# Decoded weights kept in a DRAM scratch for the paired tokens, and another order of the seven products

## The chip, the cores and the metric

The kernel runs on one NeuronCore of a Trainium2 chip. The metric is the time of one execution on the device in microseconds (us).

## What is computed

Three blocks follow one another. The inputs of the first are float32; the weights of the other two are float64 and are carried to the chip as pairs of 32-bit words, so each 128x512 block of them is 512 KB.

```python
# 16 heads (2 x 8), 768 rows, head dim 64
mask   = q_bucket[:, :, :, None] == k_bucket[:, :, None, :]   # buckets: signs of 6 projections
scores = np.where(mask, 0.125 * q @ k^T, -1e9)
x = softmax(scores) @ v                  # -> x: 1536 tokens x 512
a = x @ w1; b = x @ w2                   # 512 -> 1024 each
x = ((a * b) @ w3) @ w_out               # -> 512
g = x @ w_gate; val = x @ w_val          # 512 -> 1536 each
out = (silu(g) * val) @ w_out2           # -> 512
```

Every product is made nearly float32-exact from three matmuls: both factors are split into a high and a low half (fp32r), and `split_mm` (L248) adds high x high, high x low and low x high. A tile of 128 x 1024 columns holds the high half (columns 0 to 511) and the low half (512 to 1023).

## The kernel before

The order of the work on every engine is made by a planner (`Plan`, L57). Each piece of work is an op with a cost for each engine that may do it, a priority, the ops it waits for (`deps`), the ops that must have been started first (`after`), and counted resources that it takes and gives back (`acq`, `rel`: `W` for slots of 128 x 1024, `F` for single PSUM banks, `two` for pairs of banks, `st` for small temporaries, `D`). The planner walks through modelled time, and the program is then written out in that order, engine by engine; the semaphores come from the tiles that the instructions read and write. DMAs are issued on SP, in order, except for the casts of keys and queries on POOL; the planner lets a load start only while its modelled DMA queue is no more than 4 us deep. Matmuls outside the attention ("fill") are chained in one fixed order by `fill_op` (L821).

Weights: `decode` (L329) loads a raw block and turns the float64 bits into float32 in three steps on ACT or POOL (`e`, `l`, `s`: L341, L347, L353, recorded in the helper at L255 or L257) and a join on DVE (L360). `piece` (L381) then writes the high half (ACT first) and the low half (POOL first, L262) into a slot.

Tokens come in three blocks of 512. Block 0 goes its own way; blocks 1 and 2 are paired and handled by seven instead of eight products of half-size blocks (Strassen-Winograd). The stages in order of time:

- Attention, until about 308 us; w3 x w_out is folded into one matrix `WP` beside it (tiles `wps`).
- First mixture for block 0 (tiles `f`, `fs`; L942), with `w12f` pieces, partly beside the attention.
- Second mixture for block 0, the items stage (tiles `m` and `acc`; L923 to L938 and `stage2`): 12 items of two pieces of gate and value weights and one of output weights (`w2x`), 24 + 12 matmuls each.
- The paired tokens: `pair(1, ...)`, some 465 to 608 us, then `pair(2, ...)`, to the end.

In `pair` (L1221) four (first mixture) or six (second) steps `jp` each take two sets `z` of weights (for the two factors) from `wset` (L1125). A set loads and decodes two raw blocks again, forms the four sums s1 to s4 in place of words that are no longer needed (L1140 to L1145), and splits A, C, B (512 columns) and D (256). `xset` makes the fourteen token operands once for each stage. `PROD` (L1214) names the weight, its column and the token operand of each product; each has two halves `q` of three matmuls. Products 1 and 2 share bank `a`, 6 has `b`; 5 and then 3 use half 0 of the two-bank tile `cd`, 7 and then 4 its half 1. `after` (L1293) adds the evictions: `u` is a copy of `a` on ACT after product 1; the sums after 6, 5, 7, 3 and 4 are DVE operations at L1308 (`v` is that of product 5), each read from PSUM and added to what went before. `some()` puts one unit of the second layer (three matmuls, `pacc_...` or `acc`) between products. The order of products in all steps but the first is the list at L1507.

For the second mixture 24 more pieces (`wo2p_j`, `wo2q_j`, L1232 to L1238) load and decode the output weights, twice.

Slots go round through a first-in first-out list (`slot`, `drop`, L222 to L230).

Of the kernel before, what the change touches and what calls it, by code (L numbers as in the profile page):

```python
# [31 lines left out]
N_DEC_MOE, N_SA_MOE, N_OT = 1, 0, 2  # L32
N_D, N_ST = 3, 4
P_OUT, P_SPLIT, P_T, P_X2, N_GATE = -3, -2, -1, -2.5, 6
# [137 lines left out]
def moe_after_bucket_attention(ctx: ExitStack, tc: tile.TileContext, qk, vv, pp, cst, w12, w3t, w_out, wgv, wo2, out):  # L172
# [24 lines left out]
    def c_pool_mul(cols):  # L197
# [6 lines left out]
            "W": NSLOT - 2 - 2 * X_W - WP_W, "C": 0, "ot": 0, "R": N_R, "sums": N_SUM,  # L204
            "XT": 0, "D": 0, "st": 0, "G": 0,
        }
# [613 lines left out]

    def fill_op(name, cost, fn, deps, prio, acq=(), rel=()):  # L821
        fill_prev[0] = op(name, [("PE", cost, fn)], [*deps, fill_prev[0]], prio, acq=acq, rel=rel)
        return fill_prev[0]
# [40 lines left out]

    def stage1(key, kind, tb, wk, wdep, keep, dropx=False, late=False):

# [4 lines left out]
        for z, kc in zk:  # L871
# [57 lines left out]
    def first_stage(n):  # L929
        kind, tb, j = items[n]  # L930
        if (kind, j) not in cache:
            srcs = [(w12 if kind == 1 else wgv)[j, z] for z in range(2)] + ([wo2[j]] if kind == 2 else [])
            names = [f"w{kind}x{n}_{z}" for z in range(len(srcs))]
            cache[(kind, j)] = names, [piece(a, b, P_DEC) for a, b in zip(names, srcs)]
        used[n] = cache[(kind, j)]
        if not keep[n]:
            del cache[(kind, j)]
        return stage1(f"m{n}", kind, tb, *used[n], keep[n], n == N - 1, n == 0)  # L938


    half_done = {}
    for half in range(2):  # L942
        cdone = []
        for j in range(4 * half, 4 * half + 4):
            wk = [f"w12f_{j}_{z}" for z in range(2)]
            wd = [piece(wk[z], w12[j, z], P_DF) for z in range(2)]
            for z in range(2):
                loads[z - 2].after.append(sc[min(NTL - 1, int(F_GATE[0] + (2 * j + z) * F_GATE[1]))])
            cdone.append(stage1(f"f{j}", 1, 0, wk, wd, False))
        oj = [(o_, jj) for o_ in range(4) for jj in range(4)]  # L950
# [56 lines left out]
    tail = [o for os_ in xdone.values() for o in os_]  # L1007
    sw = op("switch", [("NONE", 0.0, switch)], tail, -50, rel=[("W", NSLOT_MOE), ("ot", N_OT), ("dec", N_DEC_MOE), ("D", N_D), ("st", N_ST)])

    def stage2(n, cdep):  # L1010
# [11 lines left out]
        for o_ in range(4):  # L1022
# [24 lines left out]
            deps = [cdep, wp_done[j] if kind == 1 else used[n][1][2], sw]  # L1047
            o = fill_op(f"s2_{n}_{o_}", C3, go, deps, nextp(), acq=[("two", 1)] if first and at[o_][1] == 0 else [], rel=rel)
            if not last:
# [47 lines left out]

    def raw2(key):
        return f(env["raw" + key]).rearrange("p (a b) -> p a b", b=2)

    def hilo(name, src, dst, deps, prio, acq=(), rel=(), make=None, done=None, n=512, engines=("ACT", "POOL", "DVE")):
# [22 lines left out]

    def wset(key, srcs):  # L1125


        oa = decode(key + "a", srcs[0], P_DEC, acq=(("W", 3),))
        ob = decode(key + "b", srcs[1], P_DEC, acq=(("W", 2), ("D", 1)))

        def add(out_, a, b, alu):
            def make(eng):
                return lambda: eng.tensor_tensor(out=out_(), in0=a(), in1=b(), op=alu)

            return [("DVE", d_dve(256), make(DVE)), ("POOL", d_pool(256), make(POOL))]

        def v(side, word, half):
            return lambda: raw2(key + side)[:, 256 * half : 256 * half + 256, word]

        a11, a12, a21, a22 = v("a", 1, 0), v("a", 1, 1), v("b", 1, 0), v("b", 1, 1)  # L1140
        s1, s3, s2, s4 = v("b", 0, 1), v("b", 0, 0), v("a", 0, 0), v("a", 0, 1)
        o1 = op("s1" + key, add(s1, a21, a22, ALU.add), [ob], P_DEC, port=BOTH)
        o2 = op("s2" + key, add(s2, s1, a11, ALU.subtract), [o1, oa], P_DEC, port=BOTH)
        o4 = op("s4" + key, add(s4, a12, s2, ALU.subtract), [o2], P_DEC, port=BOTH)
        o3 = op("s3" + key, add(s3, a11, a21, ALU.subtract), [oa, ob], P_DEC, port=BOTH)  # L1145

        def whole(x):
            return lambda: (env[x + key][:, 0:512], env[x + key][:, 512:1024])

        def blocks():  # L1150
            t = env["wB" + key]
            return tuple(t[:, c : c + 512].rearrange("p (b a) -> p b a", b=2) for c in (0, 512))

        def d_tile():
            env["wD" + key] = pools["m"].tile([128, 512], F32R, tag="D", name="D" + key, bufs=N_D)

        got = {}
        got["A"] = hilo("A" + key, lambda: raw2(key + "a")[:, :, 1], whole("wA"), [oa], P_DEC, make=lambda: slot("wA" + key))
        got["C"] = hilo(
            "C" + key, lambda: raw2(key + "a")[:, :, 0], whole("wC"), [o4, got["A"]], P_DEC, make=lambda: slot("wC" + key),  # L1160
            done=lambda: drop("raw" + key + "a"), rel=[("W", 1)],
        )
        got["B"] = hilo(
            "B" + key, lambda: raw2(key + "b")[:, 256:512, :].rearrange("p a b -> p b a"), blocks, [o1, ob], P_DEC,
            make=lambda: slot("wB" + key),
        )
        got["D"] = hilo(
            "D" + key, lambda: raw2(key + "b")[:, 0:256, 0], lambda: (env["wD" + key][:, 0:256], env["wD" + key][:, 256:512]),
            [o3, got["B"]], P_DEC, make=d_tile, done=lambda: drop("raw" + key + "b"), rel=[("W", 1)], n=256,
        )  # L1170
        return got

    def xset(kind, deps, gate, prio):
# [40 lines left out]
    PROD = {  # L1214
        1: ("A", 0, "B11"), 2: ("A", 256, "B21"), 3: ("C", 256, "B22"), 4: ("B", 256, "T4"),
        5: ("B", 0, "T1"), 6: ("C", 0, "T2"), 7: ("D", 0, "T3"),
    }
    FREES = {2: "A", 3: "C", 4: "B", 7: "D"}
    cd = [None, None, None]

    def pair(kind, nj, xdep, lead, gate, prio):  # L1221
# [8 lines left out]
        for jp in range(njp):  # L1230
            for z in range(2):
                w_of[jp, z] = wset(f"{kind}_{jp}_{z}", [(w12 if kind == 1 else wgv)[2 * jp + m, z] for m in range(2)])  # L1232
            if kind == 2:
                for j in (2 * jp, 2 * jp + 1):
                    wo_of[j] = piece(f"wo2p_{j}", wo2[j], P_DEC)
        if kind == 2:
            for j in range(nj):
                wo_of[j, 2] = piece(f"wo2q_{j}", wo2[j], P_DEC)  # L1238

        def prod(jp, z, p):  # L1240
# [5 lines left out]
            for q in range(2):  # L1246

                def go(q=q):
# [8 lines left out]
                    w, x = env[f"w{wn}{key}"], env[f"X{kind}{xn}{q}"]  # L1257
                    n = 256 if wn == "D" else 512
                    c = c0 + 128 * q
                    split_mm(ps, w[:, c : c + 128], w[:, n + c : n + c + 128], x[:, 0:512], x[:, 512:1024], begins and q == 0, q == 1, not begins)  # L1260
                    if q == 1 and p in FREES:
                        (env.pop if p == 7 else drop)(f"w{FREES[p]}{key}")
                    if jp == njp - 1 and z == 1:
# [16 lines left out]
                if q == 1 and p in FREES:  # L1280
                    rel = [("D", 1)] if p == 7 else [("W", 1)]
                if jp == njp - 1 and z == 1:
# [322 lines left out]
```

## Time and profile before

| what | value |
| --- | --- |
| median of 3 runs | 826.59 us (825.54 to 827.94) |
| the profiled execution: its time | 828.18 us |
| its span, first to last instruction | 826.4 us |
| mean granted TensorE clock | 0.993 |
| busy, share of the span: PE, weight loads, DVE, ACT, POOL | 93%, 76%, 72%, 75%, 44% |
| DMA | 107.87 MB, 131 GB/s over the span; written to HBM 3.19 MB |

Busy time of TensorE runs to the modelled end of each matmul, and successive matmuls overlap: a 128x512 matmul has a duration of 0.39 us, while its successor in a full stream starts 0.23 us after it. Time lost on TensorE is therefore read from start to start, or from the idle time of its weight loads (PEld), which run ahead of the matmuls. DMA share is the mean busy share of the 16 DMA engines.

### The profile page before, as it was taken

How to read it: one execution, taken by the hardware profiler on the slowest of the kernel's cores; microseconds unless marked ns; L12 is line 12 of the kernel's file. 1: busy time of each engine (PE TensorE's matmuls, PEld its weight loads, DVE VectorE, ACT ScalarE, POOL GpSimd, SP SyncE). 2: the span in 40 equal slices, each digit the busy share in tenths (PEclk: the TensorE clock that was granted, in tenths of full speed). 3: DMA queues.
4: the chain of work that ended last, by engine and by line, in shares of the span. 5: the costliest groups of instructions: out<-in, count | busy, mean ns of one | idle time of the engine just before them, and what ended most of it. 6: DMA issues, size and time to landing. Idle time of an engine off the chain costs nothing.

```text
span 826.4 us, 11593 instructions
## 1 busy us (share of the span) xinstructions
PE 770.3 (93%) x3888; PEld 625.7 (76%) x3888; DVE 598.3 (72%) x1014; ACT 618.4 (75%) x1105; POOL 361.3 (44%) x355
## 2 busy tenths in 40 slices
PE   7998999999999999999999979999997998998897
PEld 5886888888878897877888757677775676666686
DVE  6888878897789884676944657676866677776682
ACT  6988999987889897999778855455855666585681
POOL 3577667674755635652223112224014543333340
PEclk9999999999999999999999999999999999999999
DMA  6785956764566418642254152213142223223311
GB/s 204 171 220 136 225 159 147 159 179 123 142 175 160 126 50 320 204 151 74 75 180 154 52 182 73 76 52 103 51 153 78 101 102 102 102 102 128 128 51 52
DMA packets 35844, 107.87 MB, mean 131 GB/s; under 512 B 7060, under 2 KB 9236, under 8 KB 35784
## 3 DMA queue, kind: packets, MB, share of 16 engines
q1 hardware_dynamic: 33544, 96.11, 37.8%
q0 software_dynamic: 2240, 11.01, 6.6%
q8 instruction: 31, 0.51, 0.3%
q14 instruction: 29, 0.24, 0.1%
HBM read 97.85 MB, written 3.19 MB: 122 GB/s over the span
## 4 chain that ended last, share of the span: by engine, by line
PE 60%; ACT 14%; DVE 14%; issue 5%; POOL 3%; DMA 2%; SPq 1%; POOLq 0%; DVEq 0%; ACTq 0%
PE cd L249 6%; PE cd L251 4%; PE cd L250 4%; PE T L611 4%; DVE v L1308 3%; ACT dec_w2x L255 2%; PE pacc_two L249 2%; PE pacc_two L251 2%; PE pacc_two L250 2%; PE av L680 2%; PE av L681 2%; PE S L582 2%; PE a L249 2%; DVE sl_G L1308 2%; PE a L250 2%
## 5 line engine op out<-in xcount | busy, mean ns | idle before, releaser
L262 DVE TENSOR_TENSOR P<-T,P 128x768 fp32r<-128x768 f32 x96 | 90.9, 954 | 18.0 <-ACT P L615 16.9
L589 DVE TENSOR_SCALAR_CACHE_REDUCE ms<-S 128x768 f32<-128x768 f32 x96 | 91.4, 952 | 15.6 <-PE S L583 6.5
L602 ACT ACTIVATE ms<-ms,mx 128x768 f32<-128x768 f32 x96 | 89.8, 936 | 10.4 <-DVE mx L596 9.8
L615 ACT CAST P<-T 128x768 fp32r<-128x768 f32 x96 | 76.1, 796 | 7.2 <-PE T L611 4.9
L611 PE MATMUL T<-cs,ms 128*128 128x128 f32 x576 | 79.1, 276 | 2.4 <-DVE ms L589 1.3
L582 PE MATMUL S<-KQ 128*128 128x512 f32 x192 | 68.8, 362 | 7.2 <-DVE ms L589 3.2
L680 PE MATMUL av<-P,VP 128*128 128x256 f32 x288 | 74.4, 292 | 0.7 <-ACT P L615 0.4
L611 PEld LDWEIGHTS T<-cs,ms 128*128 128x128 f32 x576 | 65.5, 141 | 9.8 <-ACT P L615 2.4
L681 PE MATMUL av<-P,VP 128*128 128x256 f32 x288 | 71.6, 283 | 0.8 <-DVE P L262 0.8
L583 PE MATMUL S<-KH,QL 128*128 128x512 f32 x192 | 60.9, 340 | 0.7 <-DVE QL L507 0.7
L680 PEld LDWEIGHTS av<-P,VP 128*128 128x128 f32 x288 | 54.6, 190 | 2.5 <-ACT tt L691 1.4
L681 PEld LDWEIGHTS av<-P,VP 128*128 128x128 f32 x288 | 54.8, 190 | 1.7 <-DVE P L262 1.2
L582 PEld LDWEIGHTS S<-KQ 128*128 128x128 f32 x192 | 36.3, 189 | 17.8 <-DVE ms L589 5.6
L262 POOL TENSOR_TENSOR sl_w2x<-sl_raww2x,sl_w2x 128x512 fp32r<-128x512 f32 x19 | 25.2, 1330 | 43.4 <-ACT sl_w2x L255 43.4
L360 DVE SCALAR_TENSOR_TENSOR sl_raww2x<-dec_w2x,dec_w2x 128x512 uint32<-128x512 uint32 x36 | 26.8, 756 | 22.8 <-ACT dec_w2x L255 19.4
L255 ACT ACTIVATE dec_w2x<-sl_raww2x 128x512 f16<-128x512 f32 (+1 forms) x57 | 40.8, 732 | 2.2 <-DVE sl_raww2x L360 1.6
L583 PEld LDWEIGHTS S<-KH,QL 128*128 128x128 f32 x192 | 36.5, 190 | 6.1 <-DVE QL L507 1.1
L249 PE MATMUL m<-sl_X,sl_w2x 128*128 128x512 f32 x96 | 38.0, 396 | 2.5 <-ACT sa_m L893 2.5
L1336 ACT COPY u<-a 128x512 f32<-128x512 f32 x20 | 11.7, 586 | 35.5 <-PE a L251 35.4
L250 PE MATMUL m<-sl_X,sl_w2x 128*128 128x512 f32 x96 | 38.1, 397 | 0.0
L251 PE MATMUL m<-sl_X,sl_w2x 128*128 128x512 f32 x96 | 38.0, 396 | 0.0
L714 POOL TENSOR_TENSOR tt<-tt 128x256 f32<-128x256 f32 x24 | 18.1, 755 | 24.3 <-ACT tt L691 18.2
(334 smaller groups left out, 2488.5 us busy)
## 6 DMA issues: line engine op xcount, KB each, us to landing
sl_raww2x<-in_wgv_dram SPq DMA_DIRECT2D x24, 512.0 KB, 3.5
KQ<-in_qk_dram POOLq DMA_DIRECT2D x28, 384.0 KB, 6.1
sl_raww<-in_w3t_dram SPq DMA_DIRECT2D x16, 512.0 KB, 5.2
sl_raww12f<-in_w_dram SPq DMA_DIRECT2D x16, 512.0 KB, 5.7
sl_raww2x<-in_wo_dram SPq DMA_DIRECT2D x12, 512.0 KB, 4.7
sl_rawwo2p<-in_wo_dram SPq DMA_DIRECT2D x12, 512.0 KB, 3.4
sl_rawwo2q<-in_wo_dram SPq DMA_DIRECT2D x12, 512.0 KB, 4.0
kqraw<-in_qk_dram SPq DMA_DIRECT2D x28, 192.0 KB, 3.4
```

Source lines behind the costliest of these rows:

```text
L249: PE.matmul(ps, a_hi, b_hi, start=first, stop=False, skip_group_check=more)
L250: PE.matmul(ps, a_hi, b_lo, start=False, stop=False, skip_group_check=more)
L251: PE.matmul(ps, a_lo, b_hi, start=False, stop=last, skip_group_check=more)
L262: eng.tensor_tensor(out=out_, in0=a, in1=b, op=ALU.subtract)
L582: PE.matmul(ps[:, c0:c1], a[:, 0, qs], a[:, 1, c0:c1], start=True, stop=False)
L583: PE.matmul(ps[:, c0:c1], q[:, qs], k[:, c0:c1], start=False, stop=True)
L589: DVE.tensor_scalar(out=env[f"ms{s}"], in0=ps[:, 0:S], scalar1=-BIG, scalar2=None, op0=ALU.max, op1=ALU.max, accum_out=env[f"mx{s}"][:, 0:1],)
L602: ACT.activation(p, p, AF.Exp, bias=m[:, 1:2], scale=0.125, accum_out=env[f"sums{hh}"][:, qt : qt + 1])
L611: PE.transpose(ps[:, c * 128 : c * 128 + 128], p[:, c * 128 : c * 128 + 128], ident)
L615: ACT.copy(env[f"P{n}"][:, kk, 0:6], env[f"T{s}"][:, 0:S].rearrange("p (c q) -> p c q", c=6))
L680: PE.matmul(ps[:, 0:256], vab, p[:, :, c], start=c == 0, stop=False)
L681: PE.matmul(ps[:, 0:256], vab, p[:, :, 6 + c], start=False, stop=c == 5)
```

## The change

`piece` gets a `save` name: once the low half is written, SP stores the whole decoded slot (512 KB) into a DRAM scratch tile. The pieces of the first mixture for block 0 (16) and of the items stage (36) are saved; the last matmul that reads such a slot is planned after its store has been issued. `wset` no longer decodes: `fetch` loads the two saved tiles as A and B, two full sums high + low are formed in one slot F, the four sums of the set are made in place on its quarters, and F's halves are split as P (s2, s4) and Q (s3, s1). `C` and `D` go; a set now has four slots A, B, P, Q. The 24 output-weight pieces of the second mixture become 24 fetches. There are seven `st` temporaries in place of four and the three `D` tiles. In the steps after the first, product 2 moves behind product 5, and units come after 6, 2, 7 and 3 (before: 6, 5, 7 and 3).

```diff
-N_D, N_ST = 3, 4
+N_ST = 7
...
+    saved = {}
+
-    def piece(key, src, prio, late=()):
+    def piece(key, src, prio, late=(), save=None):
...
+        if save is not None:
+
+            def put():
+                env["dram" + save] = dpool.tile([128, 1024], F32, name="dram" + save)
+                SP.dma_start(out=env["dram" + save], in_=f(env[key]))
+
+            saved[save] = op("sv" + key, [("SP", 0.48, put)], [o6], -4, xfer=1.4)
         return o6
...
-            o = fill_op(f"{key}_{z}{kc}", C3, go, [wdep[z], *xdeps(kc, tb)], nextp(), acq=[("F", 1)] if kc == 0 else [], rel=rel)
+            o = fill_op(f"{key}_{z}{kc}", C3, go, [wdep[z], *xdeps(kc, tb)], nextp(), acq=[("F", 1)] if kc == 0 else [], rel=rel, after=[saved[sv[z]]] if kc == 3 else [])
...
-            cache[(kind, j)] = names, [piece(a, b, P_DEC) for a, b in zip(names, srcs)]
+            cache[(kind, j)] = names, [piece(a, b, P_DEC, save=f"{kind}_{j}_{z}") for z, (a, b) in enumerate(zip(names, srcs))]
...
-            wd = [piece(wk[z], w12[j, z], P_DF) for z in range(2)]
+            sv = [f"1_{j}_{z}" for z in range(2)]
+            wd = [piece(wk[z], w12[j, z], P_DF, save=sv[z]) for z in range(2)]
...
-    def wset(key, srcs):
-        oa = decode(key + "a", srcs[0], P_DEC, acq=(("W", 3),))
-        ob = decode(key + "b", srcs[1], P_DEC, acq=(("W", 2), ("D", 1)))
...
+    def fetch(key, save, acq, prio=P_DEC):
+        def load():
+            SP.dma_start(out=f(slot(key)), in_=env["dram" + save])
+
+        o = op(
+            "ld" + key, [("SP", 0.48, load)], [saved[save]], prio, acq=[("W", acq)], xfer=1.9, after=[last_load[0], *load_after],
+            queue=Q_LOAD,
+        )
...
+    def wset(key, a, b):
+        got = {"A": fetch("wA" + key, a, 3), "B": fetch("wB" + key, b, 2)}
+        def full(x, h):
+            def make(eng):
+                def go():
+                    if "F" + key not in env:
+                        slot("F" + key)
+                    w = f(env[f"w{x}{key}"])
+                    eng.tensor_tensor(out=f(env["F" + key])[:, HALF[h]], in0=w[:, 0:512], in1=w[:, 512:1024], op=ALU.add)
...
+            return op(f"f{x}{key}", [("POOL", d_pool(512), make(POOL)), ("DVE", d_dve(512), make(DVE))], [got[x]], P_DEC, port=BOTH)
...
+        fa, fb = full("A", 0), full("B", 1)
+        o1 = add("s1", 3, 2, 3, ALU.add, [fb])
+        o3 = add("s3", 2, 0, 2, ALU.subtract, [fa, o1])
+        o2 = add("s2", 0, 3, 0, ALU.subtract, [o1, o3])
+        o4 = add("s4", 1, 1, 0, ALU.subtract, [o2])
...
+        got["P"] = hilo("P" + key, lambda: f(env["F" + key])[:, HALF[0]], whole("wP"), [o4], P_DEC, make=lambda: slot("wP" + key))
+        got["Q"] = hilo(
+            "Q" + key, lambda: f(env["F" + key])[:, HALF[1]], whole("wQ"), [o1, o3, got["P"]], P_DEC, make=lambda: slot("wQ" + key),
+            done=lambda: drop("F" + key), rel=[("W", 1)],
+        )
...
     PROD = {
-        1: ("A", 0, "B11"), 2: ("A", 256, "B21"), 3: ("C", 256, "B22"), 4: ("B", 256, "T4"),
-        5: ("B", 0, "T1"), 6: ("C", 0, "T2"), 7: ("D", 0, "T3"),
+        1: ("A", 0, "B11"), 2: ("A", 256, "B21"), 3: ("P", 256, "B22"), 4: ("B", 256, "T4"),
+        5: ("Q", 256, "T1"), 6: ("P", 0, "T2"), 7: ("Q", 0, "T3"),
     }
-    FREES = {2: "A", 3: "C", 4: "B", 7: "D"}
+    FREES = {2: "A", 3: "P", 4: "B", 7: "Q"}
...
-                    wo_of[j] = piece(f"wo2p_{j}", wo2[j], P_DEC)
+                    wo_of[j] = fetch(f"wo2p_{j}", f"2_{j}_2", 1)
...
-                order = [(z, p) for z in range(2) for p in (1, 6, 2, 5, 7, 3, 4)]
+                order = [(z, p) for z in range(2) for p in (1, 6, 5, 2, 7, 3, 4)]
             for z, p in order:
                 prod(jp, z, p)
-                if p in (6, 5, 7, 3):
+                if p in (6, 2, 7, 3):
                     some()
```

## Rows read from the trace of the kernel before

**Rows 1.** Timeline, items stage: start us, us, engine, line, operation, tiles, [idle <-releaser].

```profile
449.01 0.39 PE L249 MATMUL m<-sl_X,sl_w2x 128*128 128x512 f32 x1
...
452.94 0.77 DVE L262 TENSOR_TENSOR sl_w2x<-sl_raww2x,sl_w2x 128x512 fp32r<-128x512 f32 x1 [0.93 <-ACT sl_w2x L255]
...
457.17 0.39 PE L249 MATMUL m<-sl_X,sl_w2x 128*128 128x512 f32 x1
```

**Rows 2.** Busy time by stretch: us, then busy (count) each, PEclk, DMA share, GB/s.

```profile
310.00:441.00 131.00, 127.34 (x558) 104.11 (x557) 80.93 (x111) 109.32 (x187) 55.06 (x48) 0.99 0.49 166
498.00:580.00 82.00, 77.31 (x318) 58.04 (x317) 56.45 (x91) 43.62 (x75) 23.86 (x23) 1.00 0.22 71
636.00:785.00 149.00, 135.31 (x547) 101.01 (x546) 106.86 (x164) 99.06 (x168) 56.29 (x55) 0.99 0.32 110
```

**Rows 3.** Waits of weight loads, 498:580, then 636:785: total us, times, longest.

```profile
PEld cd L249 <- DVE v L1308: 5.7, 7, 1.2
PEld cd L249 <- DVE sl_G L1308: 3.8, 6, 1.2
PEld cd L249 <- DVE t L1308: 1.6, 3, 0.5
PEld cd L249 <- issue: 1.2, 2, 0.6
...
PEld cd L249 <- DVE v L1308: 12.7, 15, 1.2
PEld cd L249 <- DVE sl_G L1308: 6.6, 10, 1.2
PEld cd L249 <- DVE t L1308: 4.7, 5, 1.2
```

**Rows 4.** Timeline of TensorE and DVE, one short wait and one long.

```profile
559.90 0.39 PE L251 MATMUL pacc_two<-sl_C1p,sl_WP 128*128 128x512 f32 x1
560.48 0.47 PE L249 MATMUL cd<-sl_X1T,D 128*128 128x512 f32 x1 [0.20 <-DVE v L1308]
...
642.51 0.39 PE L251 MATMUL cd<-sl_X2T,D 128*128 128x512 f32 x1
642.93 0.69 DVE L1308 TENSOR_TENSOR v<-cd,u 128x512 f32<-128x512 f32 x1 [0.82 <-PE cd L251]
643.68 0.50 PE L249 MATMUL cd<-sl_X2T,D 128*128 128x512 f32 x1 [0.79 <-DVE v L1308]
```

**Rows 5.** Weight loads for D, idle until (us, times): 498:580, then 636:785.

```profile
  DVE v L1308: 2.8, 4
  issue: 1.2, 2
...
  DVE v L1308: 8.0, 10
```

**Rows 6.** Groups from 441 us on: count, busy us, mean ns, idle, releasers.

```profile
L255 ACT ACTIVATE dec_wo2p<-sl_rawwo2p 128x512 f32<-128x512 f32 (+1 forms) x22 | 15.9, 729 | 2.4 <-DVE sl_raw_1b L360 1.2 <-DVE sl_raw_1a L360 1.0
...
L262 POOL TENSOR_TENSOR sl_wB<-sl_raw_0b,sl_wB 128x512 fp32r<-128x512 f32 x5 | 6.5, 1308 | 0.8 <-ACT sl_wB L255 0.8
```

**Rows 7.** Timeline of TensorE, late operands; last row busy time by stretch, 725.72:729.14.

```profile
467.56 0.50 PE L249 MATMUL a<-sl_X1B,sl_wA 128*128 128x512 f32 x1 [0.70 <-POOL sl_wA L257]
471.82 0.50 PE L249 MATMUL a<-sl_X1B,sl_wA 128*128 128x512 f32 x1 [0.98 <-ACT u L1336]
...
723.86 0.50 PE L249 MATMUL b<-sl_X2T,sl_wC 128*128 128x512 f32 x1 [2.08 <-ACT sl_wC L255]
...
725.72:729.14 3.42, 3.42 (x10) 2.64 (x9) 2.75 (x7) 3.08 (x5) 0.97 (x1) 0.50 0.06 22
```

**Rows 8.** Busy time, a stretch of loads and one of stores; then SP's timeline.

```profile
318.00:328.00 10.00, 10.00 (x44) 7.93 (x43) 3.44 (x6) 8.00 (x14) 4.02 (x5) 1.00 0.82 295
822.00:824.40 2.40, 0.00 (x0) 0.00 (x0) 0.58 (x1) 0.00 (x0) 0.00 (x0) 1.00 0.64 246
...
309.84 5.28 SPq L333 DMA_DIRECT2D sl_raww12f<-in_w_dram  x5
```

More of the change, by code (lines that the diff above doesn't have):

```diff
@@ L862, in moe_after_bucket_attention, with stage1 @@
         wp_done.append(o)
-    def stage1(key, kind, tb, wk, wdep, keep, dropx=False, late=False):
+    def stage1(key, kind, tb, wk, wdep, keep, dropx=False, late=False, sv=()):
         zk = [(z, kc) for z in range(2) for kc in range(4)]
@@ L937, in first_stage @@
             del cache[(kind, j)]
-        return stage1(f"m{n}", kind, tb, *used[n], keep[n], n == N - 1, n == 0)
+        return stage1(f"m{n}", kind, tb, *used[n], keep[n], n == N - 1, n == 0, [f"{kind}_{j}_{z}" for z in range(2)])
     half_done = {}
@@ L1047, in stage2 @@
             deps = [cdep, wp_done[j] if kind == 1 else used[n][1][2], sw]
-            o = fill_op(f"s2_{n}_{o_}", C3, go, deps, nextp(), acq=[("two", 1)] if first and at[o_][1] == 0 else [], rel=rel)
+            o = fill_op(f"s2_{n}_{o_}", C3, go, deps, nextp(), acq=[("two", 1)] if first and at[o_][1] == 0 else [], rel=rel, after=[saved[f"{kind}_{j}_2"]] if o_ == 3 else [])
             if not last:
@@ L1123, in hilo @@
         return op(name + "l", [("DVE", d_dve(n), lo(DVE)), ("POOL", d_pool(n), lo(POOL))], [o], prio, rel=list(rel), port=BOTH)
-    def wset(key, srcs):
-        oa = decode(key + "a", srcs[0], P_DEC, acq=(("W", 3),))
-        ob = decode(key + "b", srcs[1], P_DEC, acq=(("W", 2), ("D", 1)))
-        def add(out_, a, b, alu):
-            def make(eng):
[L1133 to L1145, printed above, removed]
+    def fetch(key, save, acq, prio=P_DEC):
[5 more added lines that the diff above has]
+        )
+        load_after.clear()
+        last_load[0] = o
+        return o
@@ new lines, in wset, with quarter, add @@
+    def wset(key, a, b):
+        got = {"A": fetch("wA" + key, a, 3), "B": fetch("wB" + key, b, 2)}
+        def full(x, h):
+            def make(eng):
+                def go():
[3 more added lines that the diff above has]
+                    eng.tensor_tensor(out=f(env["F" + key])[:, HALF[h]], in0=w[:, 0:512], in1=w[:, 512:1024], op=ALU.add)
+                return go
+            return op(f"f{x}{key}", [("POOL", d_pool(512), make(POOL)), ("DVE", d_dve(512), make(DVE))], [got[x]], P_DEC, port=BOTH)
+        def quarter(q):
+            return f(env["F" + key])[:, 256 * q : 256 * q + 256]
+        def add(name, to, x, y, alu, deps):
+            def make(eng):
+                return lambda: eng.tensor_tensor(out=quarter(to), in0=quarter(x), in1=quarter(y), op=alu)
+            return op(name + key, [("DVE", d_dve(256), make(DVE)), ("POOL", d_pool(256), make(POOL))], deps, P_DEC, port=BOTH)
+        fa, fb = full("A", 0), full("B", 1)
[3 more added lines that the diff above has]
+        o4 = add("s4", 1, 1, 0, ALU.subtract, [o2])
@@ L1147, in whole @@
         def whole(x):
             return lambda: (env[x + key][:, 0:512], env[x + key][:, 512:1024])
[L1150 to L1169, printed above, removed]
+        got["P"] = hilo("P" + key, lambda: f(env["F" + key])[:, HALF[0]], whole("wP"), [o4], P_DEC, make=lambda: slot("wP" + key))
@@ L1231, in pair @@
             for z in range(2):
-                w_of[jp, z] = wset(f"{kind}_{jp}_{z}", [(w12 if kind == 1 else wgv)[2 * jp + m, z] for m in range(2)])
+                w_of[jp, z] = wset(f"{kind}_{jp}_{z}", f"{kind}_{2 * jp}_{z}", f"{kind}_{2 * jp + 1}_{z}")
             if kind == 2:
                 for j in (2 * jp, 2 * jp + 1):
-                    wo_of[j] = piece(f"wo2p_{j}", wo2[j], P_DEC)
+                    wo_of[j] = fetch(f"wo2p_{j}", f"2_{j}_2", 1)
         if kind == 2:
             for j in range(nj):
-                wo_of[j, 2] = piece(f"wo2q_{j}", wo2[j], P_DEC)
+                wo_of[j, 2] = fetch(f"wo2q_{j}", f"2_{j}_2", 1)
         def prod(jp, z, p):
@@ L1257, in go @@
                     w, x = env[f"w{wn}{key}"], env[f"X{kind}{xn}{q}"]
-                    n = 256 if wn == "D" else 512
                     c = c0 + 128 * q
-                    split_mm(ps, w[:, c : c + 128], w[:, n + c : n + c + 128], x[:, 0:512], x[:, 512:1024], begins and q == 0, q == 1, not begins)
+                    split_mm(ps, w[:, c : c + 128], w[:, 512 + c : 640 + c], x[:, 0:512], x[:, 512:1024], begins and q == 0, q == 1, not begins)
                     if q == 1 and p in FREES:
-                        (env.pop if p == 7 else drop)(f"w{FREES[p]}{key}")
+                        drop(f"w{FREES[p]}{key}")
                     if jp == njp - 1 and z == 1:
```

14 lines of the change are left out of this document (6 added, 8 removed).

## The prediction

> **What bounds the kernel now.** I read the page first, then busy time by stage, then the waits of the weight loads and the order of time around them. TensorE is the busiest engine of the page, but the modelled ends of matmuls hide short waits, so I counted matmuls. In the items stage (gate and value weights for the unpaired tokens) the first matmuls of the last two items stand at 449.01 and 457.17 [rows 1]: 8.16 us for an item of 36, or 0.227 us from start to start. Between 310 and 441 us there is room for little more than the 558 matmuls seen [rows 2]; nothing on TensorE can be won there. In the paired stages there is: 318 matmuls in 82 us and 547 in 149 us [rows 2] are 72 and 124 us at that step, so 10 and 25 us are idle (a few records can be missing, so these are upper ends). A gain has to come from these two stretches, from the first products of each pair stage, or not at all.
>
> What the idle time waits for is plain: the weight loads of the `cd` products wait for DVE evictions, 18 times in 498 to 580 and 30 times in 636 to 785, 12.3 and 24.0 us in all [rows 3]. That is three times in each of sixteen product sets (the four sets of each stage's first pair, with another order, lie outside). There are two kinds. In the short one the matmul after a unit starts 0.58 us after its predecessor (559.90 to 560.48) instead of 0.227: 0.26 to 0.36 lost. In the long one the first three matmuls of product 7 run, then eviction `v` of product 5 (642.93, 0.69 us, itself waiting for those matmuls), and only at 643.68 the other three: 1.17 us after 642.51, so 0.94 lost [rows 4]. Product 7 writes half 1 of `cd` and `v` reads half 0. The trace therefore shows waits by the whole two-half tile, not by the half. Product, eviction, next product form one chain through 5, 7, 3, 4, with one unit of three matmuls (0.68 us) as cover.
>
> A rule speaks against this reading: the Trainium skill, PSUM — Partial Sum Buffer, section PSUM bank collisions raise a hardware error, says to guard by bank and quadrant, by which the other half would not have to wait. The trace disagrees in all 48 places (0.26 to 0.94 us each); by the rule the new distance between 5 and 7 would be worth nothing, which is the second rival below.
>
> **The change part by part.** The sum is made against the profiled execution, 828.18 us (span 826.4); that is 1.6 above the median of 826.59, which I take off at the end.
>
> (a) New order in the sets after each first pair: 1, 6, unit, 5, 2, unit, 7, unit, 3, unit, 4. Between 5 and 7 there are now nine matmuls, 9 x 0.227 = 2.0 us, where the short kind shows that an eviction needs 0.68 + 0.26 to 0.36, about 1.0. So the wait at 7 goes. Its size: weight loads for `D` waited 2.8 + 1.2 + 8.0 = 12.0 us in 16 places [rows 5]. A stalled load shows 0.26 more idle than its matmul loses, since in a full stream it runs 0.23 ahead of it (1.21 idle against 0.94 lost): 12.0 - 16 x 0.26 = 7.8 us. Between 7 and 3, and 3 and 4, there is still one unit; those 32 waits stay. Product 2 comes six matmuls later, its first use of `a` is further away, and no wait of that bank shows in these stretches [rows 3], so this costs nothing. Bank `a` is held 1.4 us longer; its next user is the next-but-one acquisition, over thirty matmuls away. Gain 7.8, bounds 0 to 8.
>
> (b) Weights from the scratch. A set loses six decode steps of 0.73 us that ACT or POOL does, two DVE joins, the splits of A and of the half tile D; each of the 24 output-weight loads loses its whole decode. In their place a set gets two full sums of 512 columns (POOL first: 1.31 us each, the nearest row [rows 6]), the same four quarter sums on contiguous halves, and two splits. Forty sums are 52 us of POOL; it has 56 of 149 us busy [rows 2], decode steps among them. None of this ends a stage, as TensorE does; it pays only where weights came late:
>  - At 723.86 product 6 waited 2.08 us for the high half of C. About 2 us after that wait the granted clock is 0.50, the lower of its levels (1.2 GHz), for 3.4 us [rows 7], half of which is lost: 1.7. TensorE had no longer hole in this stretch before it, so I count it with the wait: 3.8.
>  - At the first pair's start the second A came 0.7 us late (467.56) and product 2 waited 1.0 us for the copy of `a` (471.82) [rows 7]. A now arrives decoded, and the leading unit of 12 matmuls moves ahead of that product 2 (units run after 2, no more after 5): 1.7.
> Gain 5.5, bounds 2 to 6.
>
> (c) With less on DVE (107 of 149 us busy [rows 2]) evictions are queued less often behind decode work, and a long wait becomes a short one, 0.68 less. The 32 remaining waits hold 36.3 - 12.0 = 24.3 us; 32 x 0.52 + 0.69 n gives n = 11 long ones. A third of them: 2.4; bounds -2 to 7.5, as the written order may also get worse.
>
> (d) Stores: 52 tiles of 524 KB, 16 from the first eight pairs of weights, 36 from the items stage. Near-alone rates: loads 295 GB/s at a DMA share of 0.82, stores 246 at 0.64 [rows 8], so 360 and 384 GB/s at a full share. From 310 to 441 us, 131 us x 166 GB/s = 21.7 MB move now [rows 2]; 36 stores and some six of the others (five of their loads are issued after 309 us [rows 8]) add 22 MB: 43.7 MB, which needs 121 us at 360 GB/s. It fits by a tenth, but not evenly: three loads and three stores an item are 3.15 MB, 8.7 us at that rate against 8.16 of TensorE. The cover is the lead of decoded weights, and at the end it is thin: a low half that starts at 452.94 and ends 453.7 [rows 1] stands 3.5 us before item 11 begins. Against that, ACT no longer decodes paired weights from 441 on. I take 2 us lost, bounds 0 to 6.
>
> (e) Waits on SP. A store waits on SP for the low half (POOL 1.31 us or DVE), and later loads, key-row copies and row sums queue behind it; they feed heads and weights. Its place in the order is where the plan expects the low half, so it waits only by how far the chip lags the plan. Some eleven stores fall in the attention stage. No row shows such a wait: from 0 to 11 x 1.31 = 14 us, nearest 0, since each would have to reach TensorE. I take 1. A slot's next writer waits for the store's landing, behind a first-in first-out list of free slots, and a fetch for a store of an earlier stage: nothing.
>
> (f) Slots. A set now holds four slots, not three and a D. By the code's counts 12 circulate in the first pair stage (8 + 14, less 14 token splits, plus 4 dropped): two sets ready and the next one's A. A set of 42 matmuls with its units takes over 12 us, the preparation some 10: nothing.
>
> Sum: -7.8 - 5.5 - 2.4 + 2 + 1 = -12.7. 828.2 - 12.7 = 815.5; less 1.6, **813.9 us**.
>
> **The rivals.**
> 1. Stores saturate the DMA engines and the items stage starves (ends slower). For: 43.7 MB in 131 us is 93% of the best rate seen. Against: loads are idle half the time now, and neither kind of row is slow. No row shows both directions at once. The sign turns when the lateness eats what (a) to (c) win less (e), 14.7 us, beyond the 3.5 of cover: 131 + 3.5 + 14.7 = 149 us, so below 43.7 / 149 = 293 GB/s. At 260 GB/s it is 168 us, 168 - 134.5 = 33.5 late, less the 14.7: 826.6 + 18.8 = 845 us. Chance 0.10.
> 2. Product 7 never waited for `v`'s half but for other work that ended with it, as the rule by bank would have it, and the wait moves along: (a) is 0, 813.9 + 7.8 = 822 us. Against it is the same step in 16 places. Chance 0.06.
> 3. The new written order makes more long waits, and weights are a little late in items ((d) 6 instead of 2, (c) a loss of 2): 813.9 + 4 + 4.4 = 822, up to 825; over 824 the change is lost in the noise. Chance 0.14.
> 4. DVE is relieved so far that nearly all long waits become short: (c) 7.5, (d) 0: 813.9 - 5.1 - 2 = 807, and down to 803 with (e) and other late operands gone. Chance 0.12.
> 5. Forecast, 807 to 820: 0.58.
>
> **How the numbers follow.** Range 803 to 824: it leaves out rival 1, some of rival 3 and a little of rival 4, two in ten. About 0.3% (2.5 us) is what a measurement of this kernel can tell from no change. Faster: forecast, 2, 4 and half of 3, 0.83; same: most of the other half, 0.06; slower: rival 1 and the rest, 0.11.
>
> **What would show it.** (a) In sets after the first pair, no wait of `cd` products on T3 for `v`; waits per set two instead of three. (b) No 2 us hole with a half-clock stretch near 715 to 730, ACT in 636 to 785 at less than half of its 99 us. (c) Fewer than 11 long waits. (d) DMA share in 310 to 441 near 0.9 instead of 0.49, and matmuls there still 0.227 apart; a hole before an item's first matmul, released by a split that itself waited for a DMA, is rival 1. (e) Item 11 begins within 3 us of 457.17. The prediction fails if the items stage ends more than 5 us later, or if the paired stretches don't shrink by at least 10.

## The result

| kernel | median us (runs) | range | ratio to before |
|---|---|---|---|
| before | 826.07 (4) | 821.44 to 827.94 | |
| after | 803.69 (4) | 803.52 to 805.26 | 0.9742 [0.9699, 0.9784] |

The change wins 22.4 us, where 12.7 was forecast. The profiled execution took 803.58 us with a span of 801.8; before it was 828.18 with 826.4, so 24.6 us of span are to be explained. The first matmuls of the stages share them out (rounded). A first pair is counted up to the first unit of the pair behind it, so the first two products of that pair's first set are in it:

| stretch of the span, us | before | after | difference |
|---|---|---|---|
| start to the first items matmul | 365.7 | 366.0 | +0.4 |
| items stage | 99.7 | 96.9 | -2.8 |
| first paired stage, its first pair | 34.0 | 31.8 | -2.2 |
| first paired stage, the rest | 108.6 | 103.0 | -5.6 |
| second paired stage, its first pair | 30.1 | 31.7 | +1.6 |
| second paired stage, the rest, with the end | 188.4 | 172.3 | -16.1 |

Busy time by stretch of the kernel after (stretches and columns as in [rows 2]; the second line is a stretch not shown there):

```profile
310.00:441.00 131.00, 127.87 (x591) 105.76 (x590) 77.30 (x115) 111.21 (x191) 45.95 (x40) 1.00 0.81 284
441.00:498.00 57.00, 52.05 (x221) 40.51 (x220) 35.99 (x53) 26.60 (x46) 22.60 (x18) 1.00 0.58 205
498.00:580.00 82.00, 80.86 (x342) 62.82 (x341) 52.05 (x85) 20.06 (x35) 23.97 (x20) 1.00 0.25 80
636.00:785.00 149.00, 145.65 (x616) 113.99 (x617) 81.44 (x129) 35.87 (x61) 36.71 (x29) 1.00 0.32 110
```

Between 310 and 441 us the DMA share went from 0.49 to 0.81, and TensorE runs more matmuls than before, not fewer. In the stretch from 636 ACT fell from 99 to 36 us and DVE from 107 to 81, and TensorE fits 616 matmuls where 547 stood; some of these lie behind the last product, since the stage begins earlier now.

Waits of the weight loads of the kernel after, over the same sixteen product sets as [rows 3], which now lie at 494:571 and 629:760 (columns as there):

```profile
PEld cd L249 <- DVE sl_G L1321: 3.1, 6, 0.5
PEld cd L249 <- DVE v L1321: 1.6, 3, 0.5
PEld cd L249 <- DVE t L1321: 1.6, 3, 0.5
...
PEld cd L249 <- DVE sl_G L1321: 5.2, 10, 0.5
PEld cd L249 <- DVE v L1321: 3.5, 5, 1.4
PEld cd L249 <- DVE t L1321: 3.3, 5, 1.2
```

48 waits have become 32, two a set, and none is at product 7. I also counted from start to start on TensorE, taking off the step of 0.2275 us, and call everything above 0.55 us long. Only two are long now (the longest of the `v` and `t` lines), and one of these, 1.09 us at 649.77, stands ahead of a product's first matmul and not between its halves. Before, the 48 waits lost 23.5 us (16 long ones, five of them at product 7); after, the 32 lose 9.8.

The timeline of the kernel after shows the late operands that are left, then a short wait in full:

```profile
627.15 0.50 PE L249 MATMUL b<-sl_X2T,sl_wP 128*128 128x512 f32 x1 [1.20 <-ACT sl_wP L255]
...
628.43 0.50 PE L251 MATMUL b<-sl_X2T,sl_wP 128*128 128x512 f32 x1 [0.55 <-DVE sl_wP L262]
...
663.06 0.39 PE L251 MATMUL pacc_two<-sl_wo2p,sl_C2p 128*128 128x512 f32 x1
663.55 0.50 PE L249 MATMUL cd<-sl_X2B,sl_wP 128*128 128x512 f32 x1
663.89 0.40 PE L250 MATMUL cd<-sl_X2B,sl_wP 128*128 128x512 f32 x1
664.12 0.40 PE L251 MATMUL cd<-sl_X2B,sl_wP 128*128 128x512 f32 x1
```

A wait costs twice: 663.06 to 663.55 is 0.26 more than a step, and the next matmul stands 0.34 behind, not 0.23, another 0.11. The holes at 467.56, 471.82 and 723.86 of [rows 7] are gone or down to 0.25 (465.90). A new one, 1.37 + 0.71 us, stands at 627.15 and 628.43, where the split weights of the second paired stage's third set come late (the first set behind the first pair).

### The profile page after: what moved, and what is told of

Same layout as the page of the kernel before. It is cut to its first block, busy times and chain, and to the rows that moved or that the text cites. A ratio compares the mean times of both kernels' runs of the same rounds, so it can differ in the third digit from the quotient of the medians.

```text
span 801.8 us, 11300 instructions
## 1 busy us (share of the span) xinstructions
PE 761.0 (95%) x3888; PEld 624.9 (78%) x3888; DVE 539.3 (67%) x929; ACT 486.3 (61%) x880; POOL 332.9 (42%) x321
## 4 chain that ended last, share of the span: by engine, by line
PE 67%; DVE 13%; ACT 8%; issue 5%; DMA 4%; POOL 2%; SPq 0%; POOLq 0%; ACTq 0%; DVEq 0%
PE cd L249 6%; PE T L620 5%; PE cd L251 4%; PE cd L250 4%; PE av L689 3%; PE av L690 3%; DVE sl_G L1321 3%; PE pacc_two L249 2%; PE pacc_two L251 2%; PE pacc_two L250 2%; PE S L591 2%; PE S L592 2%; PE a L249 2%; PE a L251 2%; PE a L250 2%
## 5 line engine op out<-in xcount | busy, mean ns | idle before, releaser
L598 DVE TENSOR_SCALAR_CACHE_REDUCE ms<-S 128x768 f32<-128x768 f32 x96 | 91.3, 951 | 20.5 <-PE S L592 13.8
L689 PE MATMUL av<-P,VP 128*128 128x256 f32 x288 | 75.8, 297 | 0.6 <-ACT tt L700 0.3
L690 PE MATMUL av<-P,VP 128*128 128x256 f32 x288 | 72.6, 286 | 0.8 <-DVE P L262 0.8
L1349 ACT COPY u<-a 128x512 f32<-128x512 f32 x20 | 11.7, 586 | 72.0 <-PE a L251 71.9
L1167 POOL TENSOR_TENSOR sl_F<-sl_F 128x256 f32<-128x256 f32 x17 | 12.8, 756 | 84.8 <-DVE sl_F L1167 84.4
L262 POOL TENSOR_TENSOR sl_w2x<-sl_raww2x,sl_w2x 128x512 fp32r<-128x512 f32 x20 | 27.1, 1360 | 50.1 <-ACT sl_w2x L255 47.1
L255 ACT ACTIVATE dec_w2x<-sl_raww2x 128x512 f32<-128x512 f32 (+1 forms) x64 | 45.0, 728 | 3.9 <-DVE sl_raww2x L360 3.4
L249 PE MATMUL m<-sl_X,sl_w2x 128*128 128x512 f32 x96 | 37.5, 390 | 1.4 <-ACT sa_m L902 1.4
L251 PE MATMUL m<-sl_X,sl_w2x 128*128 128x512 f32 x96 | 37.4, 389 | 0.0
L250 PE MATMUL m<-sl_X,sl_w2x 128*128 128x512 f32 x96 | 37.3, 389 | 0.0
```

What stands on the lines that cost most here:

```text
L249: PE.matmul(ps, a_hi, b_hi, start=first, stop=False, skip_group_check=more)
L250: PE.matmul(ps, a_hi, b_lo, start=False, stop=False, skip_group_check=more)
L251: PE.matmul(ps, a_lo, b_hi, start=False, stop=last, skip_group_check=more)
L262: eng.tensor_tensor(out=out_, in0=a, in1=b, op=ALU.subtract)
L598: DVE.tensor_scalar(out=env[f"ms{s}"], in0=ps[:, 0:S], scalar1=-BIG, scalar2=None, op0=ALU.max, op1=ALU.max, accum_out=env[f"mx{s}"][:, 0:1],)
L689: PE.matmul(ps[:, 0:256], vab, p[:, :, c], start=c == 0, stop=False)
```

## The experiments

Each stands with the stretches of the table above, where they tell something. "Sets" are the sixteen behind the first pairs. A ratio is to the kernel before as timed beside that run, with its 95% interval.

**e1, the order alone.** The kernel before with the two edits of the order:

```diff
-for p in (1, 6, 2, 5, 7, 3, 4)]
+for p in (1, 6, 5, 2, 7, 3, 4)]
-                if p in (6, 5, 7, 3):
+                if p in (6, 2, 7, 3):
```

> The kernel before with the new product order and the new places of the units alone; weights are still loaded raw and decoded. Theory A (waits go by the whole cd tile, and an eviction takes about 1.0 us from the last matmul): the 16 waits before product 7 go, 7.8 us, and the long waits before products 3 and 4 stay near 11, since DVE still decodes: 818 us. Theory B (most of the gain of the changed kernel lies in the order, which also makes the long waits short): 811 us or less. Rival (the wait before 7 belongs to other work and moves along): 826 us.

Measured: 813.02 us, ratio 0.9843 [0.9801, 0.9886]. No wait at product 7; 32 waits, eight of them long, 14.0 us lost. The time lies between theories A and B. The rest of the first paired stage fell to 103.3 us and of the second to 177.0, but the first pair took 38.4 instead of 34.0. There TensorE stood idle for 2.3 us before 481.68, for an eviction, and the granted clock was then at the lower level for 13.6 us (busy time by stretch of e1):

```profile
483.00:496.60 13.60, 10.58 (x23) 6.37 (x21) 4.50 (x7) 2.85 (x5) 0.74 (x1) 0.50 0.16 57
```

So in this run the first pair holds back some of what the order wins in the sets; e1's four runs lie between 809.4 and 816.2 us. The order cut only three long waits that are not product 7's (11 to 8).

**e2, the scratch alone.** The kernel after with the old order; the diff is e1's, reversed.

> The changed kernel with the old product order and the old places of the units. Theory A: 16 waits before product 7 come back, all of the short kind (0.26 to 0.36 each) because DVE no longer decodes: 4 to 5 us, 808 us; long waits in the sixteen sets 0 to 4. Theory B: the long waits come back too: 815 us.

Measured: 809.36 us, ratio 0.9801 [0.9761, 0.9841]. All 16 waits at product 7 are back, 48 waits in all, but only two are long: 13.8 us lost instead of 23.5. That is near theory A. The scratch makes long waits short; the order removes a third of the waits. The two overlap: order alone takes 9.5 us off the waits, scratch alone 9.7, both 13.8, since a long wait can be won only once: five at product 7, and three at products 3 and 4 that the order alone shortened too.

**e3, the stores alone.** The kernel before, with the 52 stores written to the scratch and never read:

```diff
+            def put():
+                env["dram" + save] = dpool.tile([128, 1024], F32, name="dram" + save)
+                SP.dma_start(out=env["dram" + save], in_=f(env[key]))
+            saved[save] = op("sv" + key, [("SP", 0.48, put)], [o6], -4, xfer=1.4)
```

> The kernel before with the 52 stores to the scratch added, which nothing reads; raw loads, decoding and the product order stay. Theory A (stores are covered): 826 us, within 3; DMA share 0.8 in 310 to 441 us, matmuls of the items stage 0.227 us apart. Theory C (what the items stage won in the changed kernel, 3 us, comes from the stores moving the plan): 822 to 823 us. Rival (stores starve the items stage, and the changed kernel hides it): over 830 us.

Measured: 829.85 us, ratio 1.0039 [1.0015, 1.0063]. Busy time by stretch of e3:

```profile
310.00:441.00 131.00, 127.94 (x592) 105.81 (x591) 76.77 (x113) 111.39 (x191) 46.00 (x41) 1.00 0.80 283
441.00:498.00 57.00, 46.99 (x189) 36.30 (x188) 36.03 (x57) 41.20 (x73) 16.33 (x14) 0.94 0.61 220
```

The items stage did not lose; it took 96.9 us, as in the kernel after, against 99.7. The cost came later: the first pair took 40.1 us (34.0 before), since a weight that is still decoded there came late, with the lower clock behind the hole (waits of TensorE in e3, 463:504):

```profile
PE a L249 <- ACT sl_wA L255: 5.9, 1, 5.9
```

Its raw blocks were asked for late: SP issued the two loads for that second set at 458.28 and 461.32 instead of 446.49 and 449.21, behind stores that waited on SP for their low halves (17.0 us in 440 to 463). So all three theories missed: the stage won what theory C says, and the late weight then cost more. The kernel after decodes no paired weight there and keeps the gain.

**e4, cd as two one-bank tiles.** The prediction took it from the trace that waits go by the whole two-half tile. Here each half is a tile of its own; the third PSUM pair of the attention is given up when the pool is switched, to make room, and the last accumulators of the second stage use the two tiles too:

```diff
-                        if "cd" not in env:
-                            two("cd")
-                        ps = env["cd"][:, HALF[bank == "d"]]
+                        if "cd" + bank not in env:
+                            env["cd" + bank] = pools["psum_m"].tile([128, 512], F32, ...)
+                        ps = env["cd" + bank]
```

> The changed kernel with the two halves of cd as two tiles of one bank each (in the space of the third pair of banks, which the attention still uses as before). Theory A (waits by the whole tile): the 32 waits before products 3 and 4 go (30 short, 2 long: 9.5 us) and most of the waits of the first pair's sets (6 and 6 of 0.95 or so: up to 11 us): 783 to 790 us. Rival (the waits belong to the halves themselves or to other work): 804 us.

Measured: 791.35 us, ratio 0.9572 [0.9536, 0.9608]. In the sets there is no wait for `cd` at all. From the first items matmul to the end it takes 411.5 us instead of 435.8. But the attention lost 13 us: the first items matmul stands at 378.9, and so the time is just outside theory A's 783 to 790.

**e5, e4 with the attention's own turn of pairs.** The three PSUM pairs are taken in the sequence in which the kernel after took them, written out as a list, instead of in turn:

```diff
-        k = n_two[0] % 3
+        k = RING[n_two[0]]
```

> The changed kernel with each half of cd in a one-bank tile of its own, as in e4, but with the attention stage taking its three PSUM pairs in exactly the order in which the changed kernel took them (e4 took them in turn). Theory A (in e4 the attention lost 13 us by the turn of the PSUM pairs, and the paired stages won 24.3 us, first items matmul to end 435.8 to 411.5): 803.7 - 24.3 = 779.4, range 776 to 784, first items matmul at 366 as in the changed kernel. Rival B (the attention loses by something else that the separate tiles bring): it stays at e4's 791, first items matmul near 379.

Measured: 777.51 us, ratio 0.9419 [0.9393, 0.9446]. The first items matmul is at 363.6, so the turn of the pairs was the loss in e4. Busy time by stretch of e5, inside the two paired stages:

```profile
486.00:556.00 70.00, 70.00 (x309) 57.64 (x308) 48.00 (x76) 17.32 (x30) 25.86 (x22) 1.00 0.26 83
612.00:732.00 120.00, 120.00 (x527) 99.14 (x526) 75.37 (x114) 33.24 (x57) 36.13 (x29) 0.99 0.40 132
```

309 matmuls in 70 us and 527 in 120 us are 0.227 and 0.228 us each, the step of the items stage. TensorE is full here, with the same evictions by the same engine.

**e6, e5 with the old order.** The diff is e1's, reversed.

> e5 with the old order of products and units (1, 6, unit, 2, 5, unit, 7, unit, 3, unit, 4). Theory A (the order matters only because a write to one half of cd waits for the reader of the other): with two separate tiles nothing is left to win, so within 2 us of e5. Rival B (the order also helps by when weights or buffers are needed): e5 plus the 5.7 us that lay between e2 and the changed kernel (809.4 against 803.7).

Measured: 776.10 us, ratio 0.9401 [0.9376, 0.9425], span 774.9, and 775.0 in e5. Without the whole-tile wait the new order is worth nothing, and it costs nothing.

**e7, the kernel before with e5's tiles.** No scratch, old order.

> The kernel before (no scratch, old order) with each half of cd in a one-bank tile of its own and its own turn of PSUM pairs. Theory A (the scratch wins time in the paired stages through shorter waits for cd, so without those waits it has little left to win, only late weights, 4 to 5 us by the holes at 467, 471 and 724): 4 to 6 us above e5, 783 to 787. Rival B (the old decode of ACT 99 us and DVE 107 us in a stage that would now last some 133 us delivers weights late all through): 790 to 800, with new holes of TensorE that wait for weight slots.

Measured: 782.03 us, ratio 0.9469 [0.9442, 0.9496], 5.9 us above e6. The old decode keeps pace with a full TensorE but for single places; the worst, in the timeline of e7:

```profile
683.51 0.39 PE L268 MATMUL a<-sl_X2B,sl_wA 128*128 128x512 f32 x1
686.24 0.50 PE L266 MATMUL b<-sl_X2T,sl_wC 128*128 128x512 f32 x1 [2.34 <-ACT sl_wC L272]
```

This is the late high half of C of [rows 7] in another set, and 6.8 us at the lower clock follow it. So of the 50 us between before and e6, about 44 come from the tile's split and 6 from the scratch, when the split is made first; with the tile whole, the scratch alone won 16.5 (e2). Some 2.7 of the 44 lie ahead of the items stage, which begins at 363.0 instead of 365.7.

**e8, the full sums on DVE alone.** The kernel after with `("POOL", d_pool(512), make(POOL))` taken out of the choices of the full sums.

> The changed kernel with the full sums of 512 columns on VectorE alone (19 of 24 or so in the second paired stage ran on GpSimd). VectorE's load there rises from 81 by some 19 x 0.69 = 13 to 94 us of 132, 0.71, the share that the kernel before had (107 of 149, 0.72). Theory A (long waits for cd come from VectorE's load): long waits rise from 1 to about 8 of 32 as in e1, 8 x 0.68 = 5 us: 807 to 811. Rival B (they came from the long strided decode steps and joins, which are gone): long waits stay at 3 or fewer, 802 to 805.

Measured: 806.12 us, ratio 0.9759 [0.9736, 0.9782]. Busy time in 629:760 of the kernel after, of e8 and of e1:

```profile
629.00:760.00 131.00, 127.54 (x536) 98.68 (x535) 74.62 (x117) 34.21 (x58) 36.15 (x29) 1.00 0.36 121
```

```profile
629.00:760.00 131.00, 125.99 (x529) 97.48 (x528) 80.73 (x129) 35.79 (x61) 24.99 (x25) 1.00 0.37 125
```

```profile
629.00:760.00 131.00, 123.05 (x515) 95.30 (x516) 97.69 (x152) 88.25 (x153) 58.88 (x53) 1.00 0.35 115
```

DVE rose by 6 us, not by 13: the planner moved other steps to POOL. Long waits rose from 2 to 5, between the two expectations, and e1 has 8 at 98 us. DVE's load and the long waits rise together over the three, but the run does not separate the load from the long decode joins of rival B. In the sets the waits lose 11.7 us, 1.9 more than in the kernel after. The profiled run, the slowest of the four, also has 17 us at the lower clock in its first pair, behind a hole of 2.1 us at 475.95. The other three took 805.0 to 806.2 us at a mean granted clock of 0.995 to 0.996 (0.987 in the profiled one), so they had little of that. Their some 2 us over the kernel after would be covered by the 1.9 of the waits, but only the profiled run has a trace that could show it.

**e9, e1 with evictions written ahead.** In e1 DVE stands idle before the late evictions (timeline of DVE in e1):

```profile
711.95 0.69 DVE L1321 TENSOR_TENSOR sl_G<-sl_G,v 128x512 f32<-128x512 f32 x1
713.89 0.69 DVE L1308 TENSOR_TENSOR t<-cd,u 128x512 f32<-128x512 f32 x1 [1.26 <-PE cd L251]
```

What released `t` at 713.89 were matmuls of the other half, at 713.00 to 713.47, which the planner wrote ahead of the eviction. This is the long kind of [rows 4]. In e9 the planner has to write the eviction first:

```diff
+                if jp and q == 0 and p in (7, 3, 4):
+                    deps.append({7: ready.get((jp, z, 3)), 3: ready.get((jp, z, 4)), 4: cd[0]}[p])
```

> e1 (the kernel before with the new order alone) where, in the sets after each first pair, the planner may not write the first matmuls of products 7, 3 and 4 ahead of the eviction of the other half. In e1's trace VectorE stands idle before the evictions of the long waits, released by the three matmuls that the planner wrote ahead of them. Theory W (a long wait is made by the written order; VectorE's load matters only through the planner's clock): 0 or 1 long waits in these sets instead of ten, all 32 short, 813.0 - 10 x 0.68 = 806, range 804 to 809. Rival L (the eviction would have come late anyway, behind decode work on VectorE): the long waits remain as holes before the first matmul of a product, 811 to 815.

Measured: 811.06 us, ratio 0.9830 [0.9792, 0.9868]; 2 us under e1, which is less than e1's own runs differ by, and at the lower edge of rival L's range. The long form is gone: every wait now stands ahead of a product's first matmul. (In the sets e1 had eight, not the ten that the expectation counted.) But six of the 32 are still 0.61 to 1.42 us, and the 32 lose 13.1 us where e1's lose 14.0: theory W was right on the form, rival L on nearly all of the time. The longest, in e9's timeline of DVE and TensorE:

```profile
709.09 1.55 DVE L1133 TENSOR_TENSOR sl_raw_1a<-sl_raw_1b,sl_raw_1a 128x256 f32<-128x256 f32 x1
710.57 0.41 DVE L1133 TENSOR_TENSOR sl_raw_1b<-sl_raw_1a,sl_raw_1b 128x256 f32<-128x256 f32 x1
710.90 0.68 DVE L1310 TENSOR_TENSOR t<-cd,u 128x512 f32<-128x512 f32 x1
...
711.63 0.50 PE L249 MATMUL cd<-sl_X2T,sl_wB 128*128 128x512 f32 x1 [1.27 <-DVE t L1310]
```

The eviction has no idle time before it; it stood behind two decode joins, one of which took 1.55 us instead of 0.41. So the planner seems to have put the eviction late where it expected DVE to be busy, and mostly rightly. Writing it earlier won 1 of some 5 us; with the decode gone, as in the kernel after and e2, two long waits are left.

**e10, every store twice.** The kernel after, with a second store of each tile to a DRAM tile that nobody reads:

```diff
+                SP.dma_start(out=dpool.tile([128, 1024], F32, name="copy" + save), in_=f(env[key]))
```

> The changed kernel with every store issued twice, the second to a DRAM tile that nobody reads: 52 x 524 KB = 27 MB more, of which some 42 stores, 22 MB, fall into 310 to 441 us, where 37.2 MB move in the changed kernel (284 GB/s at a DMA share of 0.81). Theory A (284 / 0.81 = 350 GB/s is the ceiling for loads and stores together): 59.2 MB need 169 us instead of 131, and with a few us of lead the items stage ends some 30 to 35 late: 833 to 840. Rival B (the share of 0.81 overstates how near the ceiling is): the items stage ends within 10 us of the changed kernel's, below 815.

Measured: 827.29 us, ratio 1.0019 [0.9993, 1.0045]. Busy time by stretch of e10:

```profile
310.00:441.00 131.00, 122.93 (x563) 100.09 (x563) 69.26 (x103) 100.44 (x173) 45.66 (x41) 0.99 0.91 355
340.00:475.00 135.00, 122.90 (x515) 96.08 (x513) 76.84 (x108) 103.63 (x175) 41.32 (x34) 0.99 1.01 403
```

The first stretch is a mean: up to 340 us the DMA share is only 0.58. From 340 to 475 the DMA engines are full, at 403 GB/s and a share of 1.01 as the profile counts it. The items stage took 117.4 us instead of 96.9, and TensorE waited 4.4 us for a weight at 476. So the stage does starve, as theory A says, but the ceiling is higher than its 350 GB/s: at 403 its 59.2 MB take 147 us and not 169. With that the lateness (some 25 us with the 4 lost ahead of the stage) is less than the 30 to 35.

## Why the prediction was right, and where its sizes were off

The measured 803.7 us lies in the range of 803 to 824, but only 0.7 above its lower end and 10 under the forecast; that the range held it was a near thing. It is the case of rival 4 (chance 0.12), not the forecast's 807 to 820: the mechanisms of (a) to (c) were right, and the sum was little more than half of what was won. Terms (c) and (d) account for most of that.

**(a) The wait at product 7, -7.8: right in kind and size.** Its 16 waits lost 7.8 us before, counted from start to start, and all are gone. That the wait goes by the whole tile is shown by e4 to e6: with two tiles no wait is left, and the order no longer matters. This also settles rival 2, and with it the rule of the Trainium skill (PSUM — Partial Sum Buffer, section PSUM bank collisions raise a hardware error) to guard by bank and quadrant. e5 agrees with the rule: it guards each bank by itself and runs full. The rule doesn't describe this kernel, whose waits are set by the tile that the code names. What the step missed is the 0.11 us that a stalled matmul's successor loses too, 16 x 0.11 = 1.8 us.

**(b) Late weights, -5.5: right in kind, -4.4 net.** The hole at 723.86 with its half clock is gone (3.8 as counted before), and so are those of the first pair, which won 2.2 us where 1.7 was written. The late A went with the scratch: in e1 it is still there (466.56). The wait for the copy is gone with either part alone (e1, e2). Without the cd waits the scratch is worth 5.9 us (e6 against e7). The step didn't see the late `wP` at 627 (+1.6 net in the stretch that the table calls the second stage's first pair): a loaded weight still has to be summed and split. Here the load was not late. In POOL's and ACT's timeline the four sums of that set, by the count of the sets, end at 617.51, and its split stands on ACT right behind a copy `u` for which ACT had been idle 8 us:

```profile
614.36 3.15 POOL L1167 TENSOR_TENSOR sl_F<-sl_F 128x256 f32<-128x256 f32 x4
...
625.98 0.58 ACT L1349 COPY u<-a 128x512 f32<-128x512 f32 x1 [8.01 <-PE a L251]
626.46 0.63 ACT L255 ACTIVATE sl_wP<-sl_F 128x512 fp32r<-128x512 f32 x1
```

Whether the slot that the split writes was free earlier is not shown.

**(c) Long waits that become short, -2.4: mis-sized.** The count was right: 11 long ones among the 32 at products 3 and 4. But not a third of them turned short; nine did, and these waits fell from 15.8 to 9.8 us, -6.0. That is most of rival 4's condition. The cause it named, evictions queued behind decode work, came about in two ways. In the long kind DVE was idle and the eviction was written behind matmuls of the other half; forced ahead of them (e9), it was mostly late all the same, behind decode joins. It is the scratch that wins here, as e2 shows (2 long waits, old order), and not the new order (e1: 8); how much of it is DVE's lighter load and how much the missing joins, e8 left open.

**(d) Stores in the items stage, +2: wrong sign.** The step failed in its rate. It charged an item's 3.15 MB with 8.7 us, at 360 GB/s; at the 403 that e10 reached they take 7.8, less than TensorE's 8.16. The expected share of 0.9 was 0.81, or 0.88 at 312 GB/s from 340 us on. The matmuls keep their step: items 10 and 11 begin at 446.60 and 454.76, 8.16 us apart. So nothing was lost, and the stage got shorter by 2.8 us, at its beginning, where a wait for ACT's `sa_m` shrank. The prediction had ruled out any gain on TensorE here and missed this hole. The timeline of TensorE before, with the lower clock from the next matmul on (0.63 instead of 0.40 us):

```profile
373.85 0.55 PE L249 MATMUL m<-sl_X,sl_w2x 128*128 128x512 f32 x1 [2.53 <-ACT sa_m L893]
374.20 0.63 PE L250 MATMUL m<-sl_X,sl_w2x 128*128 128x512 f32 x1
```

The same place in the kernel after:

```profile
373.01 0.50 PE L249 MATMUL m<-sl_X,sl_w2x 128*128 128x512 f32 x1 [1.36 <-ACT sa_m L902]
373.34 0.40 PE L250 MATMUL m<-sl_X,sl_w2x 128*128 128x512 f32 x1
```

e3 has the same 96.9 us, so it comes with the stores' place in the plan, not with the loads. e1 shortened the stage too (98.1), without a store. Which step ahead of `sa_m` moved, I did not settle. Rival 1 was rightly small; its price is real, as e10 shows, but at twice the stores.

**(e) Waits on SP, +1: right in effect, wrong in its bound.** The waits are there, and longer than 1.31 us each. Of SP's waits in 225:330 of the kernel after (columns as in [rows 3]) the first line is that of the stores:

```profile
SPq L422 <- POOL sl_w12f L262: 14.7, 8, 3.7
```

They came to 14.7 us here against a bound of 14 for the whole. The last six T products of the attention begin at 317.30 instead of 308.26, and the stores do that (318.01 in e3, 308.86 in e1), but other work filled TensorE meanwhile, and the items stage begins 0.4 later. Item 11 begins at 454.76, 2.4 before its old place.

**(f) Slots, 0: right for TensorE.** The fetches do wait on SP, mostly for the last matmuls that read the slots. The largest of these waits in 441:760 of the kernel after (columns as in [rows 3]):

```profile
SPq L1136 <- PE cd L251: 122.0, 22, 12.7
```

But TensorE waited for no DMA in the paired stages, and its only late weight, the `wP` of (b), had been loaded in time.

By span: (a) -7.8, (c) -6.0, the hole at 723.86 -3.8, the items stage -2.8, the first pair -2.2, the 0.11 of sixteen waits -1.8, the late `wP` +1.6, the start +0.4: -22.4 of -24.6. The other 2 us lie in small delays that I did not assign. Of the 12 us by which the span moved further than the sum, 3.6 are (c), which was let win a third, 4.8 are (d), which was charged for a cover that did not run out, and 1.8 the second matmul behind each wait.

## What to carry to other kernels

Where a matmul waits for an eviction of something else in the same tile, first make two tiles of it: here that was worth 44 us in the kernel before (e7) and 26 in the one after (e5), of which some 2.5 lie ahead of the stages concerned, and a new order or less work on the evicting engine won only part of it. Read a long wait by what stands idle: an idle VectorE ahead of a late eviction means that the written order put it there. That does not yet say that another order wins the time: forcing it won 1 of some 5 us (e9). When two parts of a change shorten the same waits, price them together; alone they won 9.5 and 9.7 us of wait, together 13.8.

## What the runs showed of the hardware beyond what was expected

- The lower clock can cost more than its hole. In e1 and e8 a single wait of 2.3 and 2.1 us in the first pair was followed by 13.6 and 17 us at the lower level (1.2 GHz), in which the first pair's own waits went on. In e8 the first pair grew by 6.2 us over the kernel after, some 2 of them the hole itself. In the kernel after the same sets waited too, without the hole, and the granted clock stayed 1.00:

```profile
477.00:495.00 18.00, 13.15 (x51) 8.88 (x51) 9.00 (x14) 2.37 (x4) 8.09 (x9) 1.00 0.41 144
```

- Loads and stores together reached 403 GB/s at a share of 1.01, over 135 us (e10); worked out to a full share, the stretch of loads in [rows 8] gives 360 and that of stores 384. Moving both ways at once cost nothing that shows.
- The turn in which three PSUM pairs are taken moved the attention by 13 to 15 us (e4 against e5), with every matmul in the same order.
